# A hand-written instruction order for local and global attention followed by a top-k expert layer

## The chip, the cores and the metric

The kernel runs on one core of a Trainium2 chip. The metric is the device time of one launch in microseconds (us). A core has five engines with an instruction queue each: TensorE (PE, matrix products, with its weight loads shown as PEld), VectorE (DVE), ScalarE (ACT), GpSimd (POOL) and SyncE (SP, which here only issues transfers). Each queue is worked off in order. Transfers (DMA) are issued from SP's and POOL's queues and carried by 16 DMA engines that all queues share. Products land in PSUM, whose buffers here are eight banks; everything else lives in SBUF.

## The reference

Eight batches of eight heads; each head has 512 local positions and 32 global ones of 64 values. Global queries see all keys; a local query sees the 32 global keys and the local keys within 32 positions. The attention's output, 4352 rows of 512, goes through an expert layer: a gate picks one of eight experts per row, each expert keeps its 80 rows of highest gate value, and those rows get `relu(x w1) w2` times the gate; all other rows are zero.

```python
s_g = scale * q_g @ concat(k_g, k_l).T;  out_g = softmax(s_g) @ concat(v_g, v_l)
s_ll = where(abs(i - j) <= 32, scale * q_l @ k_l.T, -1e9)
out_l = softmax(concat(scale * q_l @ k_g.T, s_ll)) @ concat(v_g, v_l)
x = concat(out_g, out_l) as (4352, 512)
expert_idx = argmax(x @ w_gate); gate_w = softmax(x @ w_gate)[expert_idx]
for e in range(8):            # the 80 rows of highest gate_w of this expert
    out[tok_idx] = gate_w[tok_idx] * (relu(x[tok_idx] @ w1[e]) @ w2[e])
```

## The kernel before

The attention goes through 16 quads q: four heads of one batch, two quads to a batch, worked as two head pairs j. For a quad, `load_qk` brings Q and K (cast to fp16 by the transfer, POOL's queue), `regroup` rearranges them on ACT, `T_chunk` turns them on PE into PSUM tag T and ACT copies them to `qkT`; `S_chunk` makes three kinds of scores in PSUM tag S (G: global keys for local queries, gq: global queries, l: the band, 64 local queries against a window of 128 keys) and ACT takes their exp (`eG`, `eQ`, `eL`); DVE and POOL multiply the band's exp by a 0/1 mask `band`, one head each. `H_chunk(q, u)`, four per quad, multiplies with the values into tag O (`o_ps`, two wide products and 16 narrow ones in two passes of fp32), DVE takes the reciprocal and scales into `xn`. `Q_chunk` does the same for global queries, `X_chunk` turns `xn` through tag T into `xT` (ACT copies), and POOL casts `xn` to bf16 (`xb`). Tags T and S have two banks each, O has four. The band's odd windows read values that stand 64 rows lower, so `shift_v` makes a second copy of V by two transfers inside SBUF (SP's queue).

Once per batch, `L_chunk` computes the gate: products of `xT` with the gate's weights, a chain of small DVE steps to the gate value and the chosen expert, the rows written to `x_scr` in DRAM by SP, and a transposition of the scores. The eight batches are put in four groups; when a group is full, the 80 highest scores of each expert are found by `best`: ten rounds of MAX8 and MATCH_REPLACE per list, 53 steps in all ahead of the last merge, which `some(n)` puts between other work.

The expert weights come as pieces of 0.5 MB (cast from fp32 by the transfer, POOL's queue, 4 to an expert). Experts 0 to 2 have room from the start (12 pieces), expert 3 and half of 4 take the buffers of V when its last quads are done (6 pieces), and the other 14 take the attention's memory at its end. `zeros` fills the output with zeros (SP). After the attention come a last top-k of ten rounds, the threshold, the positions and the row indices `idx`; eight gathers of the kept rows (POOL's queue); then the experts one after the other: transpose (`xT`), `h`, relu on ACT, `y`, scaling on DVE, scatter by POOL's queue.

What sets the order: a scheduler. It takes the instructions as the code writes them down, with the loop in the last section of the listing, and reorders each engine's queue by priorities and its own model of time, so that the queues before do not follow the code. The rows of order below show where.

Of the kernel before, what the change touches and what calls it, by code (L numbers as in the profile page):

```python
# [18 lines left out]
P = 128  # L19
WIN = 32  # L20
# [6 lines left out]
def _np_consts(B, S, SG, cap):  # L27
# [6 lines left out]
    for t in range(8):  # L34
        key = 64 * t + p
        band[:, t, :] = (p - i >= 0) & (p - i <= 2 * WIN) & (key >= SG) & (key < S)
# [15 lines left out]
    c["rmask5"] = rm5  # L52
    sel = np.zeros((P, 8), dtype=np.float32)
# [11 lines left out]
def kernel(  # L65
# [14 lines left out]
    nc = tc.nc  # L80
    B, H, SL, D = q_l.shape
# [68 lines left out]

    load_gq(0, 1)
    load_qk(1)
# [36 lines left out]
    shift_v(0)  # L189
    load_gq(1, 8)  # L190
# [37 lines left out]
    def setup_globals(b0, b1):  # L228
        for t, bd in ((1, kbd), (0, qbd)):
            g_ps = psT([P, 4, 128], FP16, f"g_ps{b0}{t}")  # L230
# [506 lines left out]
```

## Time and profile before

| | before |
|---|---|
| device time, median of 3 runs | 368.97 us (365.45 to 370.99) |
| the profiled execution: device time, span | 367.61 us, 365.7 us |
| busy: PE, PEld, DVE, ACT, POOL | 260.6, 189.4, 174.4, 147.9, 147.8 us |
| mean granted clock of TensorE | 0.836 of full speed |
| transfers: POOL's queues (software), SP's (hardware) | 27.72 MB in 48.7%, 31.99 MB in 35.8% of 16 engines' span |

The profile is one execution. A stretch's row gives each engine's busy time with the number of its instructions, then the granted clock and the share of the 16 DMA engines that was busy (over 1 where packets of several queues overlap). A timeline's row gives start, length, engine, line, operation, output and inputs, and in brackets how long the engine idled before it and what it waited for.

### The profile page before, as it was taken

What the parts mean: (1) busy time and instruction counts of PE and PEld (TensorE: products, weight loads), DVE (VectorE), ACT (ScalarE), POOL (GpSimd) and SP (SyncE); (2) the same over time, 40 slices, a digit from 0 to 9 for tenths busy, and PEclk for the clock granted to TensorE, in tenths of its full rate; (3) what the DMA queues carried; (4) which work ended last, traced back from release to release, by engine and by line L of the source; (5) the groups of instructions that cost most, each with busy time, mean ns of one, the idle gap of its engine ahead of it and who ended that gap; (6) DMA issues with size and microseconds to landing.
All of it is one profiled execution on the core that took longest, in us unless ns stands there. A gap on an engine that the chain in (4) does not pass through costs nothing. (4 is left out here: it accounts for less than half of the span.)

```text
span 365.7 us, 8777 instructions
## 1 busy us (share of the span) xinstructions
PE 260.6 (71%) x3510; PEld 189.4 (52%) x3510; DVE 174.4 (48%) x553; ACT 147.9 (40%) x241; POOL 147.8 (40%) x228
## 2 busy tenths in 40 slices
PE   0368888859748989898798989499893302338993
PEld 0246675647436857756666675466671200325661
DVE  3232444606412532519854235994679797501221
ACT  2539464555707474481845647055411000001220
POOL 8814765536411642634234142115334255361211
PEclk9998989988959898898998989799896555556998
DMA  9996999999999997978585265186479999970111
GB/s 150 191 191 112 181 191 242 196 258 216 198 237 219 175 223 220 201 157 172 159 134 171 60 165 143 63 228 142 100 89 243 247 195 210 209 156 21 39 54 36
DMA packets 88601, 60.26 MB, mean 165 GB/s; under 512 B 50544, under 2 KB 79600, under 8 KB 88560
## 3 DMA queue, kind: packets, MB, share of 16 engines
q0 software_dynamic: 35040, 27.72, 48.7%
q1 hardware_dynamic: 53520, 31.99, 35.8%
q8 instruction: 27, 0.44, 0.5%
q14 instruction: 14, 0.11, 0.1%
HBM read 62.19 MB, written 14.70 MB: 210 GB/s over the span
## 5 line engine op out<-in xcount | busy, mean ns | idle before, releaser
L331 PE MATMUL o_ps<-vb,eL 128*64 128x65 f32 x1024 | 73.3, 282 | 12.7 <-DMA vb<-vb 12.7
L331 PEld LDWEIGHTS o_ps<-vb,eL 128*64 128x64 f32 x1024 | 60.3, 184 | 32.6 <-issue 21.2
L307 POOL TENSOR_TENSOR eL<-eL,band 128x512 f32<-128x512 f32 x32 | 43.8, 1369 | 32.9 <-ACT eL L305 32.6
L307 DVE TENSOR_TENSOR eL<-eL,band 128x512 f32<-128x512 f32 x32 | 29.4, 920 | 55.5 <-ACT eL L305 55.5
L366 ACT COPY xT<-x_ps 128x512 f32<-128x512 f32 x32 | 17.3, 589 | 81.1 <-PE x_ps L363 81.1
L325 PE MATMUL o_ps<-vbd,eG 128*128 128x260 f32 x128 | 43.6, 427 | 0.0
L305 ACT ACTIVATE eL<-l_ps 128x512 f32<-128x512 f32 x64 | 36.4, 596 | 14.4 <-PE l_ps L300 14.2
L140 ACT COPY qkr<-qk 128x1024 f16<-128x1024 f16 x32 | 32.6, 1043 | 11.7 <-DMA qk<-in_q_l_dram 8.0
L269 ACT COPY qkT<-T_ps 128x1024 f16<-128x1024 f16 x32 | 31.1, 1015 | 9.6 <-PE T_ps L265 9.6
L691 ACT ACTIVATE hT<-h_ps 128x320 bf16<-128x320 f32 x16 | 6.9, 437 | 63.4 <-PE h_ps L689 63.1
L300 PE MATMUL l_ps<-qkT 64*128 64x64 f16 x512 | 25.2, 194 | 7.9 <-ACT eL L305 5.0
L369 POOL CAST xb<-xn 128x1024 bf16<-128x1024 f32 x16 | 16.6, 1038 | 34.7 <-DVE xn L337 23.9
L300 PEld LDWEIGHTS <-qkT 64*128 64x128 f16 x512 | 18.9, 97 | 20.7 <-issue 18.0
L261 POOL COPY qkT<-kgp 128x32 f16<-128x32 f16 x32 | 8.7, 280 | 47.3 <-PE l_ps L300 47.1
L336 DVE RECIPROCAL rec<-o_ps 128x4 f32<-128x4 f32 x64 | 10.8, 174 | 35.2 <-PE o_ps L331 35.0
L337 DVE TENSOR_TENSOR xn<-o_ps,rec 128x256 f32<-128x256 f32 x64 | 25.1, 411 | 0.7
L325 PEld LDWEIGHTS o_ps<-vbd,eG 128*128 128x128 f32 x128 | 20.6, 200 | 2.6
L133 POOL DMA_DIRECT2D qk<-in_q_l_dram x16 | 12.7, 792 | 22.4 <-ACT qkr L140 15.8
L265 PE MATMUL T_ps<-ident,qkr 128*128 128x128 f16 x256 | 19.7, 225 | 1.4 <-DVE kgp L241 1.3
L363 PE MATMUL x_ps<-identf,xn 128*128 128x128 f32 x128 | 20.2, 288 | 0.0
L265 PEld LDWEIGHTS <-qkr 128*128 128x128 f16 x256 | 16.1, 100 | 4.8 <-issue 3.1
L697 DVE TENSOR_SCALAR y<-y_ps,xg 80x512 f32<-80x512 f32 x8 | 6.0, 747 | 26.3 <-PE y_ps L694 26.3
(137 smaller groups left out, 414.1 us busy)
## 6 DMA issues: line engine op xcount, KB each, us to landing
out_dram<-zt SPq DMA_DIRECT2D x17, 512.0 KB
vb<-vb SPq DMA_DIRECT2D x32, 260.0 KB
w2sb<-in_moe_w_dram POOLq DMA_DIRECT2D x14, 512.0 KB
vb<-in_v_l_dram SPq DMA_DIRECT2D x48, 128.0 KB
w1sb<-in_moe_w_dram POOLq DMA_DIRECT2D x12, 512.0 KB
x_scr<-xb SPq DMA_DIRECT2D x8, 514.0 KB
qk<-in_q_l_dram POOLq DMA_DIRECT2D x16, 256.0 KB
qk<-in_k_l_dram POOLq DMA_DIRECT2D x16, 256.0 KB
```

What stands on the lines that cost most here:

```text
L140: nc.scalar.copy(out=qkr[q][:, t].rearrange("p i h d -> p h i d"), in_=qks[q][:, t])
L265: nc.tensor.transpose(out=T_ps[:, t, 128 * i:128 * i + 128], in_=qkr[q][:, t, i, 2 * j:2 * j + 2, :], identity=ident16[:, :])
L269: nc.scalar.copy(out=dst.rearrange("x t (p i) -> x t p i", i=4), in_=T_ps[:].rearrange("x t (i p) -> x t p i", i=4))
L300: nc.tensor.matmul(out=l_ps[hh][:, 64 * t:64 * t + 64], lhsT=buf[o:o + 64, 512 + 64 * t:640 + 64 * t], rhs=buf[o:o + 64, 64 * t:64 * t + 6 ...
L305: nc.scalar.activation(out=eL[:], in_=l_ps[hh][:], func=AF.Exp, scale=scale)
L307: eng.tensor_tensor(out=eL[:], in0=eL[:], in1=band[:].rearrange("p t i -> p (t i)"), op=ALU.mult)
L325: nc.tensor.matmul(out=o[:].rearrange("p h d -> p (h d)"), lhsT=s["eG"][:, 128 * u:128 * u + 128], rhs=vbd[b % 2][:, qd].rearrange("p h d ...
L331: nc.tensor.matmul(out=o[64 * odd:64 * odd + 64, h, :], lhsT=s["eL"][h][:, 64 * t:64 * t + 64], rhs=v[:, 5 * odd + u, h, :], start=False, ...
L337: nc.vector.tensor_tensor(out=s["xn"][:, u].rearrange("p (h d) -> p h d", h=4), in0=o[:, :, 0:64], in1=rec[:].unsqueeze(2).to_broadcast([P ...
L363: nc.tensor.transpose(out=x_ps[:, 128 * u:128 * u + 128], in_=s["xn"][:, u, 128 * j:128 * j + 128], identity=identf[:, :])
L366: nc.scalar.copy(out=xT[:], in_=x_ps[:])
L369: nc.gpsimd.tensor_copy(out=bs["xb"][:, :, 128 * qd:128 * qd + 128].bitcast(BF16), in_=s["xn"][:])
```

## The change

`tc.manual_schedule()` takes the scheduler away: each engine's queue follows the code. The code is written anew for that. In the loop's pass q, quad q is in its last stage (H, Q, X), quad q+1 has its scores made (L, G and Q fills, mask), quad q+2 is transposed, and Q and K of quad q+3 are regrouped and of q+4 loaded; the pieces of one stage stand between the four H chunks of another. The routing of a finished batch is cut into La, Lb1, Lb2, Lb3, Lc and Ld and spread over one pass, and top-k steps go in by ones and twos: five to a pass, seven from q = 12 on. Weight pieces go out one per pass.

Some work is moved too. Q and K come as fp32 through SP's queue, and ACT casts while it regroups. The shift of V becomes two POOL copies of 64 x 1040 within the same partitions; for that the keys of each odd window stand with their halves exchanged, in a new buffer `kO` that ACT copies from `qkT` (512 columns per head pair), and the mask is exchanged likewise. The copies of `xT` go from ACT to DVE. Small fills of `L` and `oh` on POOL become a product with a constant `valid` on DVE. In the experts, transposes run one expert ahead and `y` one behind.

```diff
+    ctx.enter_context(tc.manual_schedule())
...
-        qks[q] = lpool.tile([P, 2, 4, 4, D], FP16, tag="qk16", bufs=3, name=f"qk16_{q}")
+        qks[q] = lpool.tile([P, 2, 4, 4, D], FP32, tag="qk", name=f"qk{q}")
         for t, src in ((0, q_l), (1, k_l)):
-            nc.gpsimd.dma_start(
+            nc.sync.dma_start(
...
     def shift_v(q):
-        nc.sync.dma_start(out=v[0:64, 5:9], in_=v[64:128, 0:4])
-        nc.sync.dma_start(out=v[64:128, 5:9], in_=v[0:64, 1:5])
+        nc.gpsimd.tensor_copy(out=v[0:64, 5:9], in_=v[0:64, 1:5])
+        nc.gpsimd.tensor_copy(out=v[64:128, 5:9], in_=v[64:128, 0:4])
...
+        nc.scalar.copy(out=kO[(2 * q + j) % 4][:],
+                       in_=buf[:, 576:1088].rearrange("x (u w y) -> x u w y", w=2, y=64)[:, :, ::-1, :])
...
-        nc.scalar.copy(out=xT[:], in_=x_ps[:])
+        nc.vector.tensor_copy(out=xT[:], in_=x_ps[:])
...
     for q in range(NQ):
         b, qd = divmod(q, 2)
+        more = 2 if q >= 12 else 1
+        if q + 4 < NQ:
+            load_qk(q + 4)
         if q + 2 < NQ:
             load_v(q + 2)
+        if q == 4:
+            setup_globals(4, 8)
+        G_chunk(q)
+        H_chunk(q, 0)
+        if q + 2 < NQ:
+            T_chunk(q + 2, 0)
+            kg_copy(q + 2, 0)
+        if pend is not None:
+            La(pend)
+        if q + 1 < NQ:
+            L_fill(q + 1, 0)
+            mask(q + 1, 0)
+        if q + 3 < NQ:
+            regroup(q + 3, 0)
+        if q + 1 < NQ:
             shift_v(q + 1)
+        some(1)
+        H_chunk(q, 1)
+        if pend is not None:
+            Lb1(pend)
+        if q + 1 < NQ:
+            L_fill(q + 1, 1)
+        if q + 2 < NQ:
+            T_chunk(q + 2, 1)
+            kg_copy(q + 2, 1)
+        if pend is not None:
+            Lb2(pend)
+        if q + 1 < NQ:
+            mask(q + 1, 1)
+        some(1)
+        H_chunk(q, 2)
+        if pend is not None:
+            Lb3(pend)
+        some(more)
+        if q + 1 < NQ:
+            G_fill(q + 1)
+            Q_fill(q + 1, 0)
+        if q + 3 < NQ:
+            regroup(q + 3, 1)
+        H_chunk(q, 3)
+        if pend is not None:
+            Lc(pend)
+        some(1)
+        Q_chunk(q)
+        if q + 1 < NQ:
+            Q_fill(q + 1, 1)
+        C_chunk(q)
+        X_chunk(q, 0)
+        X_chunk(q, 1)
+        some(more)
+        if pend is not None:
+            Ld(pend)
+        pend = b if qd == 1 else None
...
+        if q < 4 * NRES:
+            e, k = divmod(q, 4)
             if k == 0:
                 w_tiles(e, wpool)
             load_w(e, (k,))
...
         if q == NQ - 1:
             load_w(NRES, (2, 3))
+            load_w(NRES + 1, (0, 1))
...
+    fx(0)
+    for e in range(E):
+        if e + 1 < E:
+            fx(e + 1)
+        fh(e)
+        if e:
+            fy(e - 1)
+    fy(E - 1)
```

Three places of the order, before and after. The first is ACT's queue in one quad in the middle of the attention, before: T copies (L269), exps of the scores (L293, L286, L305), regroup (L140), xT copies (L366).

```order
L269 COPY qkT_175<-T_ps_0_1939 128x2x512
L269 COPY qkT_176<-T_ps_1_1964 128x2x512
L293 ACTIVATE eQ_0_1996<-gq_ps_0_1990 128x320
L140 COPY qkr_2404<-qk_10_2131 128x4x4x64
L305 ACTIVATE eL_0_0_2016<-l_ps_0_0_1998 128x512
L286 ACTIVATE eG_1988<-G_ps_1987 128x512
L140 COPY qkr_2404<-qk_10_2131 128x4x4x64
L305 ACTIVATE eL_0_1_2019<-l_ps_0_1_1999 128x512
L293 ACTIVATE eQ_1_2043<-gq_ps_1_2037 128x320
L305 ACTIVATE eL_1_0_2063<-l_ps_1_0_2045 128x512
L305 ACTIVATE eL_1_1_2066<-l_ps_1_1_2046 128x512
L366 COPY xT_0_2111<-x_ps_0_2106 128x512
```

The same queue of the change in one pass: L275 is the T copy, L278 the copy to kO, L322 the band's exps, L145 regroup, L293 and L303 the exps of G and gq.

```order
L275 COPY qkT_179<-T_ps_0_2005 128x2x512
L278 COPY kO_183<-qkT_179 128x512
L322 ACTIVATE eL_0_0_2035<-l_ps_0_0_2017 128x512
L322 ACTIVATE eL_0_1_2037<-l_ps_0_1_2018 128x512
L145 CAST qkr_2041<-qk_1723 128x4x4x64
L322 ACTIVATE eL_1_0_2076<-l_ps_1_0_2058 128x512
L322 ACTIVATE eL_1_1_2078<-l_ps_1_1_2059 128x512
L275 COPY qkT_180<-T_ps_1_2080 128x2x512
L278 COPY kO_184<-qkT_180 128x512
L293 ACTIVATE eG_2108<-G_ps_2107 128x512
L303 ACTIVATE eQ_0_2118<-gq_ps_0_2112 128x320
L145 CAST qkr_2041<-qk_1723 128x4x4x64
```

The T copies of the two head pairs are apart now, the first ahead of the exps of the quad before it; the xT copies are gone from ACT, and kO stands in the queue twice.

The second place is DVE's queue while a batch is routed, before: MAX (L461) and MATCH_REPLACE (L463) are the top-k rounds, the other lines the steps of L_chunk.

```order
L393 COPY L<-lg_3973 128x32
L461 MAX R_3819<-cand_3761 8x8
L394 COPY L<-lg_3973 32x8
L463 MATCH_REPLACE cand_3761<-R_3819,cand_3761 8x400
L396 TENSOR_REDUCE lmax<-L 128x5
L461 MAX R_3819<-cand_3761 8x8
L398 TENSOR_TENSOR sh<-L,lmax 128x40
```

The same steps in the change, in pass 14: L420 to L435 are the routing, L357 and L358 the division of H, L329 the band product, L499 and L501 a top-k round.

```order
L420 COPY L_191<-lg_3693 32x8
L422 TENSOR_REDUCE lmax<-L_191 128x5
L424 TENSOR_TENSOR sh<-L_191,lmax 128x40
L428 TENSOR_TENSOR oh<-L_191,lmax 128x40
L431 SCALAR_TENSOR_TENSOR cs<-rmask_148,oh 128x40
L435 SCALAR_TENSOR_TENSOR oh<-cs,oh 128x40
L329 TENSOR_TENSOR eL_1_0_3731<-eL_1_0_3731,band 128x512
L499 MAX R_3739<-cand_3674 8x8
L501 MATCH_REPLACE cand_3674<-R_3739,cand_3674 8x400
L357 RECIPROCAL rec<-o_ps_2_3742 128x4
L358 TENSOR_TENSOR xn_3623<-o_ps_2_3742,rec 128x256
```

Before, half a round stood between any two steps of the routing; now the steps follow each other, and one whole round stands ahead of the next chunk's division.

The third place is POOL's queue at the end of the attention, before: L505 and L509 issue weight pieces, L369 casts xn of a quad to xb.

```order
L505 DMA vb_71<-in_moe_w_dram 128x2x1024
L424 CAST xgb<-xgn_3114 128x128
L307 TENSOR_TENSOR eL_0_1_3651<-eL_0_1_3651,band 128x512
L413 MEMSET oh 32x8
L414 MEMSET oh 64x8
L307 TENSOR_TENSOR eL_1_1_3757<-eL_1_1_3757,band 128x512
L509 DMA vb_72<-in_moe_w_dram 128x4x512
L369 CAST xb_3578<-xn_3579 128x4x256
L509 DMA vb_72<-in_moe_w_dram 128x4x512
L505 DMA vb_70<-in_moe_w_dram 128x2x1024
L369 CAST xb_3578<-xn_3825 128x4x256
```

The same in the change: L543 and L547 issue the pieces, L392 casts, and the second CAST is that of the last quad.

```order
L392 CAST xb_3622<-xn_3623 128x4x256
L485 CAST xgb<-xgn_3155 128x128
L543 DMA vb_73<-in_moe_w_dram 128x2x1024 x2
L392 CAST xb_3622<-xn_3863 128x4x256
L547 DMA vb_74<-in_moe_w_dram 128x4x512 x2
L543 DMA vb_72<-in_moe_w_dram 128x2x1024 x2
L485 CAST xgb<-xgn_3621 128x128
L547 DMA w2sb_4058<-in_moe_w_dram 128x4x512 x2
```

Two pieces of 128x4x512 moved from ahead of the last quad's CAST to behind it; the 14 late pieces follow, as before, and the gathers come behind them in both.

## Rows read from the trace of the kernel before

**Rows 1.** The page's slices: PE's busy tenths and its granted clock.

```profile
PE   0368888859748989898798989499893302338993
...
PEclk9998989988959898898998989799896555556998
```

**Rows 2.** Stretches of one quad each: length, engines' busy time, clock, DMA share, GB/s.

```profile
core 0: us, PE busy (x) PEld busy (x) DVE busy (x) ACT busy (x) POOL busy (x), PEclk, DMA share, GB/s
68.00:89.00 21.00, 15.95 (x230) 12.58 (x229) 7.46 (x27) 9.96 (x17) 10.69 (x16) 0.84 1.19 233
141.00:155.00 14.00, 12.32 (x185) 9.86 (x185) 5.55 (x14) 8.30 (x13) 6.33 (x8) 0.88 0.85 182
155.00:172.40 17.40, 16.02 (x212) 11.26 (x211) 8.85 (x33) 9.14 (x15) 6.29 (x11) 0.90 0.79 167
216.30:240.00 23.70, 18.66 (x220) 12.93 (x219) 16.89 (x61) 9.25 (x15) 4.56 (x10) 0.86 0.41 107
267.60:275.00 7.40, 6.75 (x121) 4.96 (x120) 6.47 (x26) 1.85 (x4) 3.15 (x4) 1.00 0.96 133
```

**Rows 3.** Stretches of one microsecond in a quad, same columns.

```profile
178.00:179.00 1.00, 0.39 (x8) 0.36 (x8) 0.32 (x1) 1.00 (x2) 0.21 (x1) 1.00 0.94 361
179.00:180.00 1.00, 0.26 (x5) 0.20 (x5) 0.28 (x1) 1.00 (x3) 0.00 (x0) 1.00 0.26 102
...
182.00:183.00 1.00, 1.00 (x22) 1.00 (x20) 1.00 (x4) 0.50 (x2) 1.00 (x2) 0.50 0.00 0
```

**Rows 4.** Timeline of PE, in the hole and in two full-clock places.

```profile
179.74 0.31 PE L290 MATMUL gq_ps<-qbd,qkT 128*128 128x64 f16 x5 [1.04 <-ACT eL L305]
180.23 0.80 PE L300 MATMUL l_ps<-qkT 64*128 64x64 f16 x16 [0.18 <-ACT eL L305]
...
242.14 0.66 PE L325 MATMUL o_ps<-vbd,eG 128*128 128x260 f32 x2
...
245.20 1.15 PE L331 MATMUL o_ps<-vb,eL 128*64 128x65 f32 x28
```

**Rows 5.** Timeline from the last quad on: pieces, last X, indices, experts, last y.

```profile
266.69 0.80 POOL L509 DMA_DIRECT2D vb<-in_moe_w_dram  x1 [3.10 <-PE og L347]
...
273.25 1.09 PE L363 MATMUL x_ps<-identf,xn 128*128 128x128 f32 x8
...
317.03 0.16 DVE L666 TENSOR_TENSOR idx<-idf,inv_ps 80x8 uint32<-80x8 f32 x1
...
325.52 0.53 PEld L679 LDWEIGHTS <-xg 80*128 80x128 bf16 x8 [8.82 <-issue]
...
345.60 1.31 PE L689 MATMUL h_ps<-xT,vb 128*128 128x80 bf16 x32 [0.78 <-DVE xT L682]
...
359.52 0.75 DVE L697 TENSOR_SCALAR y<-y_ps,xg 80x512 f32<-80x512 f32 x1 [2.33 <-PE y_ps L694]
```

**Rows 6.** DMA view, 280 to 316 us: packets, MB, share of 16 engines, by queue.

```profile
q0 software_dynamic: 4749, 6.19, 100.3%
q1 hardware_dynamic: 1094, 1.60, 14.2%
```

**Rows 7.** The start: POOL's cast of quad 0, and the first 20 us.

```profile
40.76 1.04 POOL L369 CAST xb<-xn 128x1024 bf16<-128x1024 f32 x1 [1.01 <-DVE xn L337]
...
0.00:20.00 20.00, 3.22 (x24) 2.18 (x24) 5.12 (x28) 7.72 (x8) 15.94 (x39) 1.00 1.33 173
```

**Rows 8.** Groups by line and shape: busy us, mean ns, idle before.

```profile
L305 ACT ACTIVATE eL<-l_ps 128x512 f32<-128x512 f32 x64 | 36.4, 596 | 14.4 <-PE l_ps L300 14.2
...
L269 ACT COPY qkT<-T_ps 128x1024 f16<-128x1024 f16 x32 | 31.1, 1015 | 9.6 <-PE T_ps L265 9.6
...
L369 POOL CAST xb<-xn 128x1024 bf16<-128x1024 f32 x16 | 16.6, 1038 | 34.7 <-DVE xn L337 23.9 <-issue 8.9 <-DVE rg L353 0.9
...
L461 DVE MAX8 R<-cand 8x8 f32<-8x400 f32 x20 | 11.2, 561 | 0.0
```

**Rows 9.** The second half of the attention as one stretch, columns of rows 2.

```profile
141.00:274.30 133.30, 118.24 (x1674) 86.93 (x1673) 77.95 (x263) 67.05 (x111) 45.17 (x64) 0.90 0.63 142
```

**Rows 10.** DVE's band product, 141 to 216 us: ns shortest/median/longest.

```profile
L307 DVE TENSOR_TENSOR eL<-eL,band x10: 683/694/2350, 147.5 to 212.3; 128x512 f32<-128x512 f32 x10
```

More of the change, by code (lines that the diff above doesn't have):

```diff
@@ L34, in _np_consts @@
     for t in range(8):
-        key = 64 * t + p
-        band[:, t, :] = (p - i >= 0) & (p - i <= 2 * WIN) & (key >= SG) & (key < S)
+        w = p if t % 2 == 0 else (p + 64) % P
+        key = 64 * t + w
+        band[:, t, :] = (w - i >= 0) & (w - i <= 2 * WIN) & (key >= SG) & (key < S)
     c["band"] = band
@@ L52, in _np_consts @@
     c["rmask5"] = rm5
+    ok = np.ones((P, NB), dtype=np.float32)
+    ok[SG:, 4] = 0.0
+    c["valid"] = ok
     sel = np.zeros((P, 8), dtype=np.float32)
@@ L184, in shift_v @@
         v = vb[q % 3]
-        nc.sync.dma_start(out=v[0:64, 5:9], in_=v[64:128, 0:4])
-        nc.sync.dma_start(out=v[64:128, 5:9], in_=v[0:64, 1:5])
+        nc.gpsimd.tensor_copy(out=v[0:64, 5:9], in_=v[0:64, 1:5])
+        nc.gpsimd.tensor_copy(out=v[64:128, 5:9], in_=v[64:128, 0:4])
     load_v(0)
-    shift_v(0)
-    load_gq(1, 8)
+    for t in range(2):
+        regroup(0, t)
+    load_qk(1)
     load_v(1)
@@ L453, in L_chunk, with Ld @@
             nc.vector.tensor_copy(out=scT[g][:, k * P:(k + 1) * P], in_=t_ps[:])
-        return g if b == GROUPS[g][-1] else None
+        if g < 3 and b == GROUPS[g][-1]:
+            work.append(best(g))
+    def Ld(b):
+        bs = bst.pop(b)
+        xgb = spool.tile([P, 2, 64], BF16, tag="xgb", name="xgb")
+        nc.gpsimd.tensor_copy(out=xgb[:], in_=bs["xg"][:])
+        xr = x_dram.ap()[b * S:(b + 1) * S, :]
+        nc.sync.dma_start(out=xr[SG:S, :].rearrange("(u p) d -> p u d", p=P), in_=bs["xb"][:])
+        for h4 in range(4):
+            nc.sync.dma_start(
+                out=xr[0:SG, 0:XW - 1].rearrange("g (q f d) -> f g q d", q=2, f=4)[h4],
+                in_=xgb[32 * h4:32 * h4 + 32].bitcast(FP32))
+        nc.sync.dma_start(out=xr[0:SG, XW - 1:XW], in_=bs["gate"][0:SG, 4:5])
     scT, R = {}, {}
@@ L519, in zeros @@
                 nz[0] += 1
-    regroup(0)
-    setup_globals(0, 1)
-    T_chunk(0, 0)
-    T_chunk(0, 1)
-    S_chunk(0, 0)
-    S_chunk(0, 1)
-    pending = None
     work = []
     def some(n):
-        for _ in range(n):
-            if work:
-                try:
-                    next(work[0])()
-                except StopIteration:
-                    work.pop(0)
+        while n and work:
+            try:
+                next(work[0])()
+                n -= 1
+            except StopIteration:
+                work.pop(0)
@@ new lines @@
+    for t in range(2):
+        nc.vector.tensor_copy(out=gq16[:, t], in_=gqf[:, t])
+    T_chunk(0, 0)
+    setup_globals(0, 1)
+    load_qk(2)
+    for t in range(2):
+        regroup(1, t)
+    T_chunk(0, 1)
+    for j in range(2):
+        kg_copy(0, j)
+        L_fill(0, j)
+        mask(0, j)
+    shift_v(0)
+    for j in range(2):
+        T_chunk(1, j)
+        kg_copy(1, j)
+    load_qk(3)
+    G_fill(0)
+    for j in range(2):
+        Q_fill(0, j)
+    for t in range(2):
+        regroup(2, t)
@@ L609 @@
     rpool = ctx.enter_context(tc.tile_pool(name="route", bufs=1, reuse_waits="tile"))
+    xg = [rpool.tile([cap, XW], FP32, name=f"xg{e}") for e in range(E)]
+    for e in range(E):
+        nc.gpsimd.memset(xg[e], 0.0)
     lst = rpool.tile([16, cap], FP32, name="lstf")
@@ L675, with fx @@
                                      bounds_check=N - 1, oob_is_err=False)
-    for e in range(E):
+    xTs, hTs = {}, {}
+    def fx(e):
         xT_ps = psT([P, 4, cap], BF16, f"xT_ps{e}")
```

205 lines of the change are left out of this document (92 added, 113 removed).

## The prediction

> **What bounds the kernel now.** The page's slices come first: PE is 80 to 90% busy through the attention (slices 3 to 30), yet its granted clock keeps falling below full speed, and from slice 31 PE idles while weights still arrive [rows 1]. So there are two stages, the attention up to the last X transposes (274.3 us) and a tail of 91.4 us to the end of the span at 365.7, and I read each by itself.
>
> Attention, the table of one stretch per quad [rows 2]. A quad without routing work takes 14.0 us, one that carries the batch's routing (the L part) 17.4. Busy time times granted clock is PE's work at full speed: 12.32 x 0.88 = 10.8 and 16.02 x 0.90 = 14.4, mean 12.6 of 15.7. The 3.1 us between are a hole and its after-effect, and both are in the one-microsecond stretches: PE is busy for 0.39 and 0.26 of two neighbouring microseconds, and three later the granted clock is 0.50, the lower of its two levels, 1.2 GHz, and the stretch below full speed lasts some 3.3 us [rows 3]. What PE waits for in the hole is ACT: in the timeline a matmul into PSUM tag S waits 1.04 us for the exp that empties a bank of it [rows 4]; S has two banks and every score goes through it. Beside this rhythm three quads are far longer: two of some 21 us, of which one stands in the table, at a DMA share of 1.19 (all 16 engines full), and one of 23.7 us from 216.3 on, where DVE is busy 16.89 us: there the top-k rounds stand between the steps of the L part (the order rows of DVE) [rows 2].
>
> Tail, the timeline from 273 us [rows 5] and the DMA view [rows 6]. Routing has its row indices at 317.2, and the first transposes of gathered rows start only at 325.52. From 280 to 316 POOL's queue alone is busy 100.3% of 16 engines and moves 6.19 MB: weight pieces (0.524 MB each on the side written), 11.8 of them, 3.05 us each. The gathers stand behind them in the same queue. So the experts start when the last weight piece is through, 51.2 us after the attention, for the 16 pieces that POOL issues behind the last quad (16 x 3.05 = 48.8). The experts take 34.0 us to the last y (359.52) and 6.2 us are left for its scatter and the end.
>
> **The change part by part, against the profiled execution** (span 365.7, its time 367.61, which is 1.4 us below the median of the runs shown).
>
> *Start.* The qk loads come as fp32 on SP's queue instead of as a cast on POOL's, and the V shift is a POOL copy instead of two transfers. Before, quad 0 ends with its CAST at 40.8 us, and the first 20 us are DMA-bound (share 1.33) [rows 7]. The second qk pair now waits on SP for regroup(0), since its buffer is shared, and some 18 small loads stand on SP between it and the third pair, which ACT's regroup(2) needs ahead of quad 0's stage for quad 2. I take 42 us for the end of quad 0, bounds 36 (no load waits) and 48 (one regroup late by the 5 to 6 us that three pairs of 1 MB need at the 0.2 MB/us of that stretch).
>
> *Steady quads.* What now stands on PE between two fills of tag S is half of quad q's H work. On ACT the order is T copy, kO copy, two exps (the order rows of ACT). From the last transposes on that is 1.02 + 0.60 (kO has 512 columns, as an exp) + 2 x 0.60 = 2.8 us [rows 8], and I add 0.2 for the handover. PE covers it with the first score fill, 0.80 us, and H(q,1), two wide products (0.66) and 16 narrow ones (28 took 1.15) [rows 4], some 2.0 us together. So a wait of about 1 us stays in each quad; in a routing quad L work covers it, but there a matmul for tag T waits as long for the T copy. I take 1.1. Bounds: no wait, and today's 2 us. Since the wait is half of the old hole and has no second one beside it, I take the clock to stay at its upper level (2.4 GHz): 12.6 + 1.1 = 13.7 us per quad. ACT gains kO and loses xT, two copies of 512 columns each per quad: nothing in the sum. POOL gains two copies of 64x1040 per quad, 1.04 us each by the CAST of 1024 columns [rows 8], bounds 0.9 and 2.1 (as slow as its band product in the worst case), and loses two DMA issues: hidden, since POOL was busy 45.17 us of 133.3 in the second half [rows 9]. The DMA loses the 32 transfers of the shift and nothing else, qk being the same bytes read; the weight pieces come one per quad, where the order before lets POOL issue them as early as buffers allow. That takes away the stretches with share 1.2, and so the two quads of 21 us. On SP the row writes of a batch, which wait for DVE's gates and a POOL cast at a quad's end, now stand ahead of the next qk load; what queues behind them is needed by ACT a quad later, 13 us off, which hides it, and costs PE the delay one to one if they come more than that late.
>
> *Second half, DVE.* It was busy 77.95 us between 141 and 274.3 [rows 9]. It gets 16 xT copies, about 0.6 each (priced by ACT's 512 columns, bounds 0.4 and 0.9), and five more top-k rounds by then, a MAX8 of 0.56 and a replace about as long: 78 + 9.6 + 5.6 = 93 us over 8 quads, 11.7 per quad. That is under 13.7, so DVE doesn't bound, but its queue is in order and each round ahead of a reciprocal holds H's bank. I add 1.5 us to each of the 7 last steady quads, 10 us; bounds 0 and 3 each.
>
> One row speaks against the shift on POOL: the band product on DVE takes 0.69 us in the median and 2.35 at most [rows 10], in stretches where POOL multiplies too. The new copies put 2.1 us more of POOL's SBUF work beside the second band product of each quad. The Trainium skill, "SBUF - State Buffer", section "SBUF: two separate sides", says that a DVE instruction with two SBUF inputs and a GpSimd instruction take one port pair by an exclusive lock, so that the later one waits for the whole of the other. The maximum of that row agrees with it. By the row's median the copies cost nothing, and by the rule 1 to 2 us of DVE per quad. Without the page: if the second product is stretched like the longest one, DVE has 11.7 + 1.7 = 13.4 us per quad, as much as PE; that is a rival below.
>
> So the attention ends at 42 + 14 x 13.7 + 8 (the last quad has no successor; 7.4 before [rows 2], and three rounds more) + 10 = 252 us, against 274.3.
>
> *Tail.* POOL's order decides (the order rows of POOL). Both w2 pieces of expert 3 stand behind the last quad's CAST, where before they went out from 266.7 on [rows 5]: 18 pieces after the attention instead of 16. 18 x 3.05 = 55, plus 1.5 to the first issue, plus 4 for two zero fills and the last rows' write (in the DMA view 1.60 MB of SP's queue took 14.2% of 36 us, 5.1 us [rows 6]; bounds 0 and 5): the experts start 60.5 us after the attention, 9 later than now. Routing doesn't show: by then its 43 us (274.3 to 317.2) are over, even with the seven rounds that are left over for after the L part. The experts in a pipeline lose the waits of PE for xT, 0.78 us per pair of experts and some smaller ones [rows 5]: 34.0 - 2.5 = 31.5. The end stays at 6.2. Together 252 + 60.5 + 31.5 + 6.2 = 350.2 us of span, 352.1 with the 1.9 us around it. The median may lie a microsecond above: I say 352.
>
> **Rivals.**
> 1. *All waits are covered* and DVE's queue holds nobody: 42 + 14 x 12.6 + 8 = 226, so 326, and 340 when half of the waits and of DVE's 10 us stay. For it speaks that PE has work for 12.6 us only [rows 2]; against it the two banks of tag S [rows 4].
> 2. *The clock still falls.* A hole of 1.1 us per quad is enough. Each quad then pays half of 3.3 us at 1.2 GHz, 1.65 x 14 = 23: 375, and 363 when it happens in every second quad. Against it: the rows show the fall behind two microseconds that are two thirds empty [rows 3].
> 3. *POOL's copies hold DVE* (above): DVE at 13.4 us per quad with its queue waits, some 1.5 us more in 8 quads, 12 us: 364.
> 4. *Slower: top-k steps in DVE's queue stop PE.* One mechanism: in the second half a step stands ahead of each reciprocal, H runs out of its four banks, Q and X slip, and the next quad starts late; four routing quads would then cost like the 23.7 us quad, 8.7 more each, 35 us: 387. For it speaks that quad's row; against it that now one or two rounds stand in a place, where there 13 did. It turns the verdict from 3 us on each of the 8 quads.
>
> **How the numbers follow.** Forecast (343 to 361) 0.47; rival 1 0.15; rival 2 0.14; rival 3 0.12; rival 4 0.12. About 2% is what a measurement of this kernel can tell from no change (361.6 to 376.3). Faster: 0.47 + 0.15 + 0.05 of the rivals 2 and 3 = 0.67. Slower: rival 4 and a little of rival 2, 0.14. Same: 0.19. The range 334 to 375 leaves out the fastest part of rival 1 and rival 4; the likeliest case alone is 343 to 361.
>
> **What would show it.** Right: routing and other quads near 15.5 and 12 us in stretches, PEclk 1.0 between 45 and 240 us, a PE wait for ACT of about 1 us at the score fill, no DMA share of 1.2 before 140 us, the last X near 252, the first expert 60 us behind it, and POOL's queue full all that time. Wrong: a clock of 0.5 once per quad (rival 2), a band product on DVE of 1.7 us or more in each quad (rival 3), PE waiting on DVE's reciprocals from quad 8 on (rival 4), or experts that start less than 55 us after the attention.

## The result and the profile after

The changed kernel takes 338.74 us (median of 4 runs, 337.43 to 340.6) against 368.75 us: ratio 0.922, 95% interval 0.913 to 0.930. It is faster, as forecast, and 13 us better than the 352 forecast: inside the range of 334 to 375, but below the 343 to 361 of the likeliest case. Ratios compare runs outside a slower state of the chip; of the four runs with V's shift by DMA (below) only the fastest lies outside it. The profiled execution took 337.43 us; its span is 335.5. By the forecast's own stages:

| stage | forecast, us | measured, us |
|---|---|---|
| quad 0 ends | 42 | 41.9 |
| quads 1 to 7 | 7 x 13.7 = 95.9 | 82.0 |
| quads 8 to 15, to the last X | 95.9 + 8 + 10 = 114 | 119.1 |
| last X to the first expert | 60.5 | 54.8 |
| experts, to the start of the last y | 31.5 | 26.2 |
| from there to the end | 6.2 | 11.4 |

The sum is right to 4%, but with errors of both signs in it: 14 us too much for quads 1 to 7, while the other errors, 5 or 6 us each, cancel almost to nothing. The page's slices of the changed kernel first, which answer to [rows 1]:

```profile
span 335.5 us, 8730 instructions
...
PE   1206989887889889788684878769551013049960
...
PEclk9998699999999999989898599995855555559996
DMA  7787899699899899999879714204999999960211
```

From slice 6 to slice 17 the clock stays up, and PE is busy 70 to 90% (the first eight quads end in slice 15). From slice 18 on both are ragged again. The stretches show the same (columns of [rows 2]: length, busy time of PE, PEld, DVE, ACT and POOL, granted clock, DMA share, GB/s): first the two parts of the attention, then a plain quad and a routing quad of the first, then two routing quads of the second.

```profile
41.90:123.90 82.00, 72.03 (x1358) 52.97 (x1358) 54.30 (x155) 59.74 (x98) 50.05 (x60) 1.00 0.96 224
123.90:243.00 119.10, 91.66 (x1473) 63.96 (x1471) 96.07 (x283) 54.29 (x92) 51.33 (x62) 0.89 0.72 171
...
64.40:75.60 11.20, 10.19 (x221) 7.91 (x210) 6.86 (x18) 8.34 (x14) 7.33 (x10) 1.00 0.96 239
75.60:89.80 14.20, 11.28 (x190) 7.59 (x192) 11.15 (x38) 8.87 (x15) 7.17 (x9) 1.00 1.06 230
150.60:166.50 15.90, 11.60 (x194) 8.18 (x198) 14.00 (x41) 8.62 (x14) 7.08 (x9) 0.95 1.05 265
182.90:201.40 18.50, 15.40 (x206) 10.23 (x206) 13.66 (x44) 9.08 (x15) 6.69 (x8) 0.75 0.52 119
```

In the first part a quad takes 11.7 us, 10.3 of them PE work at full clock. In the second it takes 14.9, with DVE busy 12.0 and no more work for PE (91.66 us at a clock of 0.89, 10.2 per quad). The view of waits names the new holder. The first two rows are PE's waits from 41.9 to 140 us, which is eight quads, the last one those from 140 to 243 (total us, times, longest):

```profile
PE l_ps L318 <- ACT eL L322: 4.0, 8, 0.7
...
PE o_ps L352 <- POOL vb L188: 1.4, 1, 1.4
...
PE x_ps L384 <- DVE xn L358: 11.4, 8, 2.0
```

The tail answers to [rows 5, 6]. The timeline shows the last X transposes, the row indices, the first transposes of gathered rows, the first y and the last y, and the first two scatters and the last; the DMA view is of 243 to 300 us:

```profile
241.69 1.33 PE L384 MATMUL x_ps<-identf,xn 128*128 128x128 f32 x5 [1.94 <-DVE xn L358]
...
286.03 0.16 DVE L751 TENSOR_TENSOR idx<-idf,inv_ps 80x8 uint32<-80x8 f32 x1
...
297.84 0.74 PE L763 MATMUL xT_ps<-identbf,xg 80*128 80x80 bf16 x8 [12.04 <-DMA xg<-x_scr,idx]
...
304.41 0.75 DVE L785 TENSOR_SCALAR y<-y_ps,xg 80x512 f32<-80x512 f32 x1 [2.80 <-PE y_ps L782]
...
324.07 0.75 DVE L785 TENSOR_SCALAR y<-y_ps,xg 80x512 f32<-80x512 f32 x1 [0.98 <-PE y_ps L782]
...
305.44 0.95 POOL L787 DMA_INDIRECT out_dram<-y,idx  x1 [6.26 <-DVE fxT L766]
308.91 0.93 POOL L787 DMA_INDIRECT out_dram<-y,idx  x1 [2.52 <-DVE fxT L766]
...
329.22 0.91 POOL L787 DMA_INDIRECT out_dram<-y,idx  x1 [2.46 <-issue]
```

```profile
q0 software_dynamic: 7801, 10.05, 100.2%
q1 hardware_dynamic: 1208, 1.69, 9.6%
```

The indices are ready 43.2 us after the attention (42.9 before); the gathers land 54.8 us after it, when POOL's queue has moved its 18 pieces. The y's then come every 3.0 us, but the scatters only every 3.4 (8 of them, 305.44 to 329.22), and the last is issued 5.2 us behind the start of its y.

### The profile page after: what moved, and what is told of

Same layout as the page of the kernel before. It is cut to its first block, busy times and chain, and to the rows that moved or that the text cites. A ratio compares the mean times of both kernels' runs of the same rounds, so it can differ in the third digit from the quotient of the medians.

```text
span 335.5 us, 8730 instructions
## 1 busy us (share of the span) xinstructions
PE 218.9 (65%) x3510; PEld 155.6 (46%) x3510; DVE 207.6 (62%) x597; ACT 146.4 (44%) x241; POOL 149.3 (44%) x200
## 5 line engine op out<-in xcount | busy, mean ns | idle before, releaser
L329 POOL TENSOR_TENSOR eL<-eL,band 128x512 f32<-128x512 f32 x32 | 40.9, 1278 | 42.5 <-ACT eL L322 41.0
L329 DVE TENSOR_TENSOR eL<-eL,band 128x512 f32<-128x512 f32 x32 | 27.4, 855 | 41.0 <-ACT eL L322 41.0
L275 ACT COPY qkT<-T_ps 128x1024 f16<-128x1024 f16 x32 | 32.6, 1018 | 42.9 <-PE T_ps L271 37.9
L352 PEld LDWEIGHTS o_ps<-vb,eL 128*64 128x64 f32 x1024 | 37.1, 143 | 26.1 <-issue 20.6
L352 PE MATMUL o_ps<-vb,eL 128*64 128x65 f32 x1024 | 46.5, 234 | 2.4 <-POOL vb L188 1.4
L322 ACT ACTIVATE eL<-l_ps 128x512 f32<-128x512 f32 x64 | 34.7, 597 | 9.6 <-PE l_ps L318 9.6
L145 ACT CAST qkr<-qk 128x1024 f16<-128x1024 f32 x32 | 33.4, 1046 | 12.2 <-DMA qk<-in_q_l_dram 10.7
L777 ACT ACTIVATE fhT<-h_ps 128x320 bf16<-128x320 f32 x16 | 6.9, 437 | 64.0 <-PE h_ps L775 63.6
L392 POOL CAST xb<-xn 128x1024 bf16<-128x1024 f32 x16 | 16.6, 1036 | 29.7 <-DVE xn L358 29.6
L271 PE MATMUL T_ps<-ident,qkr 128*128 128x128 f16 x256 | 22.8, 240 | 10.6 <-ACT qkr L145 7.5
L384 PE MATMUL x_ps<-identf,xn 128*128 128x128 f32 x128 | 22.1, 309 | 11.4 <-DVE xn L358 11.4
L358 DVE TENSOR_TENSOR xn<-o_ps,rec 128x256 f32<-128x256 f32 x64 | 27.2, 425 | 3.2
L318 PE MATMUL l_ps<-qkT 64*128 64x64 f16 x256 | 14.5, 200 | 16.1 <-POOL qkT L283 10.0
L384 PEld LDWEIGHTS x_ps<-identf,xn 128*128 128x128 f32 x128 | 15.8, 156 | 13.9 <-DVE xn L358 13.5
L387 DVE COPY xT<-x_ps 128x512 f32<-128x512 f32 x32 | 20.6, 684 | 2.2 <-PE x_ps L384 1.9
L187 POOL COPY vb<-vb 64x1040 f32<-64x1040 f32 x16 | 17.0, 1062 | 10.4 <-DMA vb<-in_v_l_dram 10.4
L303 ACT ACTIVATE eQ<-gq_ps 128x320 f32<-128x320 f32 x32 | 13.9, 435 | 16.6 <-PE gq_ps L300 16.5
L318 PEld LDWEIGHTS <-qkT 64*128 64x128 f16 x256 | 10.2, 99 | 22.9 <-issue 11.2
```

What stands on the lines that cost most here:

```text
L187: nc.gpsimd.tensor_copy(out=v[0:64, 5:9], in_=v[0:64, 1:5])
L271: nc.tensor.transpose(out=T_ps[:, t, 128 * i:128 * i + 128], in_=qkr[q][:, t, i, 2 * j:2 * j + 2, :], identity=ident16[:, :])
L275: nc.scalar.copy(out=dst.rearrange("x t (p i) -> x t p i", i=4), in_=T_ps[:].rearrange("x t (i p) -> x t p i", i=4))
L318: nc.tensor.matmul(out=l_ps[hh][:, 64 * t:64 * t + 64], lhsT=lhsT, rhs=buf[o:o + 64, 64 * t:64 * t + 64], start=True, stop=True)
L322: nc.scalar.activation(out=eL[:], in_=l_ps[hh][:], func=AF.Exp, scale=scale)
L329: eng.tensor_tensor(out=eL[:], in0=eL[:], in1=band[:].rearrange("p t i -> p (t i)"), op=ALU.mult)
```

## The experiments

Each runs the changed kernel with the edit shown; times are medians with lowest and highest, ratios are against the kernel before on the same chip. By stage, in the profiled execution of each:

| run | to last X | to first expert | from there to end | first scatter behind first expert |
|---|---|---|---|---|
| changed kernel | 243.0 | 54.8 | 37.7 | 7.6 |
| without the fixed order | 269.1 | 49.6 | 44.5 | 12.9 |
| xT on ACT | 239.5 | 55.0 | 38.8 | 8.4 |
| places behind each move | 228.3 | 58.4 | 43.8 | 13.4 |
| w2 of expert 3 early | 248.8 | 51.9 | 39.3 | 9.0 |
| tail edits | 244.5 | 45.4 | 44.5 | 14.1 |
| attention edits | 229.4 | 55.3 | 38.1 | 8.1 |
| both | 227.8 | 48.5 | 46.9 | 14.0 |
| both, gathers spread | 229.0 | 48.5 | 41.1 | 9.3 |

**The order alone.**

```diff
-    ctx.enter_context(tc.manual_schedule())
```

> The changed kernel with the line taken out that holds each engine to the written order; the code and all data paths (V shift on POOL, fp32 qk loads on SP, the two odd-block copies, xT on DVE) stay. Theory A, the order itself pays: with another order on PE and ACT quads 1 to 7 go from 11.7 us back to 13.5 or more, the granted clock falls below 1.00 in most quads, attention ends at 262 or later, the whole takes 355 or more. Theory B, the data paths pay: quads 1 to 7 stay within 0.4 us of 11.7 and the whole is under 345.

Measured 364.79 us (364.51 to 365.76), ratio 0.989 (0.985 to 0.994). Theory A: with these data paths, 26 of the 30 us are the order's. The slice row of the clock, and two stretches, quads 2 to 7 and quads 8 to 15:

```profile
PEclk9999999969999989899789969969995555557995
```

```profile
63.85:155.44 91.59, 80.47 (x1255) 57.62 (x1252) 52.48 (x143) 64.11 (x103) 41.81 (x51) 0.93 0.79 213
155.44:269.10 113.66, 96.04 (x1477) 71.42 (x1475) 84.89 (x266) 53.40 (x91) 52.46 (x59) 0.91 0.52 133
```

Quad 1 ends at 63.85 us, not 52.7 (PE once waits 9.8 us for a transfer of global values, ahead of 41.24 us), and quads 2 to 7 take 15.3 us each, not 11.9. The clock falls less often than theory A had it (0.93, slices 9, 15 and 17). In the second half, however, 113.7 us stand against 119.1: there the written order is no better than the scheduler's. By its place the gain is all in the start, the first half and the experts.

**Score matmuls head by head.**

```diff
-        for t in range(8):
-            for hh in range(2):
+        for hh in range(2):
+            for t in range(8):
```

> The changed kernel with the 16 small score matmuls of a fill issued head by head (8 and 8), not in turns between the two heads. In the trace 16 in turns take some 0.40 us (two at once, on the two halves of TensorE's rows), while in the kernel before 8 of one head took 0.40. Theory A, part of my over-sized PE work is this: the fills take 0.8 us each, PE busy grows by 0.8 us per quad, quads 1 to 7 go from 11.7 to 12.3 or more, the second half (paced by DVE) stays, the whole goes from 338.7 to 342 to 345. Theory B, ACT's chain paces the first half: nothing beyond 1 us changes.

Measured 338.19 us (337.37 to 340.21), ratio 0.917 (0.911 to 0.923): theory B. Quads 1 to 7 take 81.6 us:

```profile
41.90:123.46 81.56, 73.28 (x1348) 54.12 (x1347) 53.74 (x153) 59.60 (x98) 49.82 (x61) 1.00 0.96 225
```

PE is busy 1.3 us longer in these seven quads, 0.2 each and not 0.8, and it goes into the wait for ACT at the same fill. The price of taking turns between the heads was not what I had over-sized.

**The V shift by DMA again.**

```diff
-        nc.gpsimd.tensor_copy(out=v[0:64, 5:9], in_=v[0:64, 1:5])
-        nc.gpsimd.tensor_copy(out=v[64:128, 5:9], in_=v[64:128, 0:4])
+        nc.sync.dma_start(out=v[0:64, 5:9], in_=v[0:64, 1:5])
+        nc.sync.dma_start(out=v[64:128, 5:9], in_=v[64:128, 0:4])
```

> The changed kernel with the V shift put back as two SBUF-to-SBUF transfers per quad (here on SP's queue) in place of the two POOL copies. Theory A, the shift's transfers were what made PE wait in the kernel before (12.7 us in 3 waits between 40.8 and 155 us): the DMA share of the first half rises above 1.1, PE waits 8 us or more for vb, the whole takes 346 to 352. Theory B, one weight piece per quad leaves the transfers room: PE waits under 2 us for vb and the whole stays within 2 us of 338.7.

Measured 383.63 us (374.93 to 389.8) against 369.49 (366.76 to 370.75). By its waits theory A, and beyond its numbers; its DMA share above 1.1 did not come (0.92 from 43.8 to 140.4 us). The run to compare is the fastest, 374.93; the profile is of the one of 386.2. PE's waits from 42 to 291 us in it, and the largest entry of SP's:

```profile
PE o_ps L352 <- DMA vb<-vb: 38.7, 8, 8.8
...
SPq L487 <- DVE xb L454: 45.3, 6, 16.4
```

With this fixed order PE stood eight times for a late transfer. SP's queue, in which the transfers stand, waits for the row writes of a batch, while the DMA share is below that of the kernel before (1.14 from 40.8 to 155 us): that points at the queue, but no run took transfer time and queue apart. So order and data path need each other: V's old data path in the new order is not faster than the kernel before (374.93 at best, one run), and the new data paths in the scheduler's order gain 1%, too little to count as a change. The other moved work (Q and K through SP, `kO`, `valid`, the experts' code) was not undone one by one.

**No top-k step in the quads.**

```diff
     def some(n):
+        if n < 9:
+            return
```

> The changed kernel with no top-k step between the parts of the quads: all 53 steps run after the last routing part. Theory A, the steps in DVE's queue are what makes quads 8 to 15 take 14.75 us each against 11.7: attention ends near 221 instead of 243 (12 us per quad); the 44 steps that move cost some 45 us on DVE behind it plus two waits for a transfer, so the whole takes some 365. Theory B, the second half is slow for something else (xT on DVE, POOL beside DVE, the clock): attention ends at 238 or later and the whole takes 380 or more.

Measured 374.23 us (2 runs). The attention ends at 223.2, quads 8 to 15 take 12.5 us each (expected 12): theory A for the attention. The whole misses its 365.

```profile
123.50:223.20 99.70, 87.08 (x1473) 62.35 (x1471) 55.52 (x168) 54.66 (x92) 50.84 (x61) 0.91 0.86 192
```

The steps in DVE's queue therefore cost the second half 119.1 - 99.7 = 19.4 us. Behind the attention they cost more, since there nothing covers them: the indices come 102 us after it.

**xT on ACT, and empty places behind the move.** Two ways to take some 11.5 us from DVE's second half.

```diff
-        nc.vector.tensor_copy(out=xT[:], in_=x_ps[:])
+        nc.scalar.copy(out=xT[:], in_=x_ps[:])
```

> The changed kernel with the xT copy (128x512, 0.68 us on DVE, two per quad) put back on ACT. Theory A, DVE's total load paces the second half: DVE loses 1.3 us per quad, quads 8 to 15 go from 14.75 to 13.7 us each, and the attention ends near 235 instead of 243; the first half may lose up to 4 us since ACT's copies and exps are what its score fills wait for; the whole 331 to 336. Theory B, not the load but the places of the top-k steps in DVE's queue stop PE: the second half changes by less than 3 us, and the whole is 337 or more.

```diff
             yield move
+            for _ in range(6):
+                yield lambda: None
```

> The changed kernel with six empty places put between the move of a group's candidates (a transfer on SP's queue) and the first top-k step that reads them. Theory A: the one wait of 4.46 us in which DVE stands before 173.98 us for that transfer, with everything behind it in its queue, goes, and the attention ends 3 to 5 us earlier; the six steps that this leaves for the tail hide there, where routing is done 11.8 us before the gathers have landed; the whole 334 to 336. Theory B: the time returns at the next steps, since DVE has its work to do in any case, and the whole stays within 1.5 us of 338.7.

Measured 335.98 us (334.99 to 339.73), ratio 0.918 (0.909 to 0.927), and 333.71 us (332.37 to 336.69), ratio 0.911 (0.903 to 0.919). The second half of the attention in the one and the other:

```profile
123.00:239.50 116.50, 92.49 (x1473) 64.78 (x1471) 84.90 (x267) 63.89 (x109) 51.22 (x62) 0.88 0.73 172
```

```profile
123.50:228.30 104.80, 85.23 (x1473) 60.39 (x1470) 84.34 (x252) 54.31 (x92) 51.11 (x61) 0.95 0.77 178
```

DVE is busy 84 to 85 us in both, 11 to 12 less than in the changed kernel. Without the xT copies that is worth 2.6 us, with the places 14.3; they leave 30 top-k rounds there instead of 41. So DVE's load alone does not pace the second half; what stands in its queue ahead of H's reciprocals does more. The xT theory B held for the second half (2.6 us, under its 3), while the whole came out 1 us below its bound, inside theory A's 331 to 336. The gap gave 14.7 us in the attention, more than its theory A said (3 to 5), and two thirds went back: 3.6 us by the longer routing and 6.1 behind the first expert. The one wait that the gap removes is this one of the changed kernel, a transfer on SP's queue for which DVE stood, and with it everything behind:

```profile
173.98 0.57 DVE L499 MAX8 R<-cand 8x8 f32<-8x400 f32 x1 [4.46 <-DMA cand<-lst]
```

The quad around it shrank from 16.4 to 10.6 us, and the last quad, with two rounds instead of eight, from 11.9 to 7.4. With xT on ACT the same wait grew to 7.5 us, so it took back part of what the copies had freed.

**Two pieces out of the tail.**

```diff
-            load_w(NRES, (0, 1))
+            load_w(NRES, (0, 1, 2, 3))
         if q == NQ - 1:
-            load_w(NRES, (2, 3))
```

> The changed kernel with both w2 pieces of expert 3 issued at the end of the last quad but one, as before the change, so that 16 and not 18 weight pieces stand behind the last quad. Theory A, POOL's queue sets when the experts start: they start 2 x 3.05 = 6.1 us sooner (48.7 us after the attention, against 54.8), the whole 332 to 333.5. Theory B, routing and the gathers' own transfers set it: under 2 us.

Measured 338.71 us (336.86 to 341.9), ratio 0.920 (0.913 to 0.927): no gain. The tail did get 2.9 us shorter, but in the profiled execution, the longest of the four, the attention was 5.8 us longer with the same instructions up to its last quads. Inconclusive by itself; the tail edits below ask it again.

**Every second scatter left out** (the rows of experts 0, 2, 4 and 6 stay zero).

```diff
+        if e % 2 == 0:
+            return
         nc.gpsimd.indirect_dma_start(out=out,
```

> The changed kernel without the scatters of experts 0, 2, 4 and 6 (their rows of the output stay zero). Theory A, the scatters run one behind the other, 3.4 us each, and set the end: with every second one gone the last follows its y at once (324.8 us in the trace), the span ends near 331, the whole is 333 to 335. Theory B, the experts' matmuls set the end: the last scatter comes where it did, the whole stays within 1.5 us of 338.7.

Measured 334.11 us (2 runs), span 331.5; the last y starts at 324.89 us and the last scatter is issued at 325.92. Theory A: the chain of scatters sets the end.

**Tail edits, attention edits, both.** Tail: w1 of expert 3 a quad earlier, its w2 behind the last quad but one, and the w2 pieces of expert 7 behind the gathers (the added line stands there):

```diff
-        load_w(e, (2, 3))
+        if e < E - 1:
+            load_w(e, (2, 3))
...
+    load_w(E - 1, (2, 3))
```

> The changed kernel with other places for eight weight pieces only: w1 of expert 3 goes out a quad earlier, its w2 behind the last quad but one, and the two w2 pieces of expert 7 behind the gathers in POOL's queue. So 14 pieces stand between the attention and the gathers, not 18. Theory A, POOL's queue sets the experts' start until routing does: 14 x 3.05 = 43 us, routing 43 us and 3.3 us for a gather to land; the experts start 46.5 us behind the attention and not 54.8, the whole takes 330 to 331. Theory B, the transfers that leave the tail lengthen the attention by as much: the attention ends at 247 or later, the whole takes 335 or more.

Attention: xT on ACT as above, four places behind the move, and

```diff
-GROUPS = [[0, 1, 2, 3], [4, 5], [6], [7]]
+GROUPS = [[0, 1, 2], [3, 4, 5], [6], [7]]
```

> The changed kernel with three edits to the attention: xT on ACT, groups of three and three batches for the first two top-k lists instead of four and two (the first list's steps begin two quads earlier), four empty places behind each move of candidates. The tail is left. Theory A, quads 8 to 15 are as long as DVE's queue makes them: DVE loses 10 us by the copies and some 12 us of steps to the quads 6 to 8, so the second half goes from 119 us to some 100 and the attention ends near 225; the experts still start 54.8 us behind it, by POOL's queue; the whole takes 318 to 323. Theory B, something else paces the second half too: the attention ends at 233 or later and the whole takes 328 or more.

> The edits of the tail and of the attention together. Theory A: the attention ends near 225, behind it routing decides (43 us, four more top-k steps of 1.05 us, 3.3 us for a gather): the experts start at 275, the whole takes 313 to 317. Theory B, the 14 pieces hold the gathers again, or the pieces moved forward slow the last quads: the whole takes 320 or more.

Measured: tail 336.85 us (336.19 to 338.73), ratio 0.916 (0.909 to 0.923); attention 325.66 us (322.14 to 326.86), ratio 0.883 (0.873 to 0.892); both 325.59 us (323.93 to 326.32), ratio 0.883 (0.876 to 0.890). All three totals miss theory A (330 to 331, 318 to 323 and 313 to 317); the first and the last lie where their theories B had them, but not for those reasons (the attention ends at 244.5 us, and the 14 pieces do not hold the gathers). The attention's edits do most of what was expected of them (229.4 us, not 225). The tail's bring the first expert to 45.4 us, as theory A said (46.5), and yet nearly nothing: the experts give it back. PE in the run with the tail edits alone, and one row each of DVE and ACT:

```profile
291.48 2.33 PE L778 MATMUL h_ps<-fxT,w1sb 128*128 128x80 bf16 x32
293.88 1.07 PE L778 MATMUL h_ps<-fxT,w1sb 128*128 128x80 bf16 x13
295.70 0.43 PE L778 MATMUL h_ps<-fxT,w1sb 128*128 128x80 bf16 x4 [0.75 <-issue]
297.14 0.49 PE L778 MATMUL h_ps<-fxT,w1sb 128*128 128x80 bf16 x5 [1.00 <-issue]
298.57 0.83 PE L778 MATMUL h_ps<-fxT,w1sb 128*128 128x80 bf16 x10 [0.94 <-issue]
299.19 3.61 PE L785 MATMUL y_ps<-w2sb,fhT 128*80 128x512 bf16 x8
...
298.69 0.33 DVE L769 COPY fxT<-xT_ps 128x320 bf16<-128x320 bf16 x1 [6.64 <-remote]
...
298.63 1.24 ACT L780 ACTIVATE fhT<-h_ps 128x320 bf16<-128x320 f32 x3 [3.84 <-remote]
```

Expert 1's products stand in three gaps that no semaphore in the profile explains, in the time in which POOL issues the last gathers (287.17 to 297.1); then y runs at half clock (3.61 us, 1.90 later). PE is not alone: DVE's copy and ACT's relu start 4.6 and 4.8 us after PE had finished their inputs (294.1 and 293.8 us), with no releaser but "remote". In the changed kernel PE starts only when the gathers are nearly all issued, and has no such gap.

**The gathers spread**, on top of both (`gather(e)` is the indirect transfer of one expert's rows).

```diff
-    for e in range(E):
+    for e in range(5):
         gather(e)
...
             fy(e - 1)
+            if e + 4 < E:
+                gather(e + 4)
```

> The kernel with the edits of the tail and of the attention, and the gathers of experts 5, 6 and 7 moved behind the scatters of experts 0, 1 and 2 in POOL's queue, so that POOL issues five gathers and not eight while the first experts run. In the run with both edits the experts started 5.5 us sooner behind the attention than in the one with the attention's edits alone, but the first scatter came 14.0 us behind their start instead of 8.1: the matmuls of expert 1 stand in three gaps of 0.8 to 1.0 us for which the profile names no releaser, while POOL still issues gathers. Theory A, what holds PE there goes with the gathers: three fewer shorten it by some 3.8 us, the first scatter comes 10 to 11 us behind the start, the whole takes 320 to 323. Theory B, the gaps belong to the first experts whatever POOL does: the first scatter comes 13.5 us or more behind the start and the whole stays within 1.5 us of 325.6.

Measured 322.68 us (320.36 to 325.74), ratio 0.877 (0.868 to 0.886). Theory A: PE's gaps are gone, and DVE's copy follows PE at once, at 281.98 us; ACT's first relu still starts 3.0 us behind the start of its products (1.3 in the changed kernel).

```profile
279.08 2.33 PE L783 MATMUL h_ps<-fxT,w1sb 128*128 128x80 bf16 x32
281.21 0.47 PE L771 MATMUL xT_ps<-identbf,xg 80*128 80x80 bf16 x4
281.48 2.33 PE L783 MATMUL h_ps<-fxT,w1sb 128*128 128x80 bf16 x32
283.61 2.06 PE L790 MATMUL y_ps<-w2sb,fhT 128*80 128x512 bf16 x8
```

The first scatter comes 9.3 us behind the first expert instead of 14.0. So the gaps hang on when POOL issues the three gathers (the two pieces behind them moved forward with that, and one execution of each was profiled); by which way they hold PE, DVE and ACT is open. This is the fastest version found by its median, and its interval lies below that of the changed kernel. Against the run with both edits the whole gains 2.9 us, with ranges that overlap.

## Why the prediction was right, and which steps were off

*Quads 1 to 7 (14 us too long).* The failed step is "Busy time times granted clock is PE's work at full speed ... mean 12.6"; measured are 10.3, and 2.3 in seven quads is more than the whole error. The pair of stretches it used was too high. Quads 1 to 7 as one stretch of the kernel before give 94.03 x 0.87 / 7 = 11.7:

```profile
40.80:155.00 114.20, 94.03 (x1345) 70.23 (x1344) 43.28 (x136) 60.82 (x97) 53.51 (x80) 0.87 1.14 215
```

and [rows 9], nine quads and not eight, gives 118.24 x 0.90 / 9 = 11.8. So the choice of stretch explains 0.9 of the 2.3. The rest is the method: busy time times clock is not fixed work, for the same products took less in the changed kernel, 72.03 / 7 = 10.3. The largest part is H's narrow products, of the same number and shape, before and after (busy us of the whole kernel, mean ns, idle before):

```profile
L331 PE MATMUL o_ps<-vb,eL 128*64 128x65 f32 x1024 | 73.3, 282 | 12.7 <-DMA vb<-vb 12.7
...
L352 PE MATMUL o_ps<-vb,eL 128*64 128x65 f32 x1024 | 46.5, 234 | 2.4 <-POOL vb L188 1.4
```

In quads 1 to 7 they were busy 34.17 us before and 19.21 after. Part of that is the clock, which was low just where they stood: multiplied by the granted clock of each half microsecond, the 34.17 are 24.4, and the other 5.2 us are 0.7 per quad. The scores l and G and the gate's products lost 0.4 to 0.5 per quad each, by the same count (busy times overlap, so these do not add up exactly). At the gate it can be seen: before, its eight products of a batch stood in two lots (the first two rows), now in one (the third, of the changed kernel), for half the time. Why the other products cost less was not tested.

```profile
159.06 1.04 PE L380 MATMUL lt_ps<-xT,wg 128*32 128x512 f32 x2
...
160.38 1.06 PE L380 MATMUL lt_ps<-xT,wg 128*32 128x512 f32 x6
```

```profile
55.06 1.07 PE L403 MATMUL lt_ps<-xT,wg 128*32 128x512 f32 x8 [0.38 <-DVE xgT L400]
```

The other half of that step was right: the wait at the score fill is there (0.5 us a quad by the view of waits, all idle time 1.4, forecast 1.1), and the clock stays up, but only to 124 us and not to 240. Rival 2 is out for these quads; in the second half the clock fell again (0.75 in one quad), and what that alone cost was not taken apart. Rival 1 comes near with its 340, but by luck: PE's waits are there, and DVE's queue holds. The shift on POOL took 1.04 to 1.05 us a copy in the median, as priced, and cost PE 1.4 us once. But I priced the removed transfers only by the DMA share; the 12.7 us that PE waited for them in three waits of the first half of the kernel before I had not looked up, and the third experiment shows what hangs on them.

*Quads 8 to 15 (5 us too short).* The mechanism was right, "each round ahead of a reciprocal holds H's bank"; its term was mis-sized. The steps cost 19.4 us, not 10 (2.4 per quad, within the bounds of 0 and 3). Of these, 4.5 us are DVE's wait for the moved candidates, which the forecast did not list. How the rest divides is not shown: spread evenly over 41 rounds, the wait and eleven rounds would be worth 8.5 us, and the gap gave 14.3 in this half. The base came out at 99.7 us without steps, against 103.9, which hid nearly half of the error. The load argument ("11.7 per quad. That is under 13.7, so DVE doesn't bound") named the wrong quantity: with equal loads, 84 to 85 us, the second halves differ by 11.7 us. It also divided the load of nine quads [rows 9] by eight; by nine it is 10.4, measured are 12.0. Rival 4 is this same mechanism, at a lower price than it asked.

*Rival 3* is real and small. DVE's band product takes 0.69 us in the median and 1.45 at most, 27.4 us in 32 where 32 x 0.69 is 22.1: 5 us in the whole kernel, and the longest is shorter than the 2.35 of [rows 10]. Before, the same 32 took 29.4 us, so the new copies made it no worse.

*Tail (5.7 us too long).* "plus 1.5 to the first issue, plus 4": 18 x 3.05 = 55 is the whole wait, since the first piece goes out at 242.68 us, before the last X is done. SP's 1.69 MB went beside the pieces, as [rows 6] had already shown, where the two queues' shares add up to 114%.

*Experts and end (37.7 forecast, 37.7 measured, by chance).* The pipeline saves 7.8 us, not 2.5: an expert takes 3.0 us. "The end stays at 6.2" failed: with y every 3.0 us the scatters, 3.4 each, become the bound, and 5.2 us come back at the end.

## What to carry to other kernels

Size an engine's work from the whole of a stage, not from two stretches next to each other, and where the clock was low in it expect less once the order changes (11.7 against 10.3 here); and price a step in an in-order queue by what stands behind it, not by its share of the load. When a stage gets faster, look up the rate of the next chain behind it (here the scatters, 3.4 us each against 3.0), and count waits for transfers from the waits view even where the DMA share seems to explain them. A fixed order paid here where every producer was early by design; with V's late transfers in it PE waited 38.7 us for them, against 12.7 in the kernel before.

## What the runs showed of the hardware

A small DVE instruction can last as long as the POOL instruction beside it. Three DVE rows and two POOL rows of the changed kernel:

```profile
221.16 0.19 DVE L428 TENSOR_TENSOR oh<-L,lmax 128x40 f32<-128x40 f32 x1
221.38 1.00 DVE L431 TENSOR_TENSOR_SCAN cs<-rmask,oh 128x40 f32<-128x40 f32 x1
222.42 1.28 DVE L435 SCALAR_TENSOR_TENSOR oh<-cs,oh 128x40 f32<-128x40 f32 x1
...
221.24 1.05 POOL L188 COPY vb<-vb 64x1040 f32<-64x1040 f32 x1
222.38 1.27 POOL L329 TENSOR_TENSOR eL<-eL,band 128x512 f32<-128x512 f32 x1
```

The scan (0.24 us elsewhere) and the product behind it (0.20 elsewhere) both have two SBUF inputs and end with POOL's instruction. The Trainium skill, "SBUF — State Buffer", section "SBUF: two separate sides", says that such a DVE instruction and a GpSimd one that reads SBUF take a shared port pair as an exclusive lock; these rows agree with it.

The other surprise is PE's three gaps of 0.75 to 1.0 us without a releaser while POOL issued gathers, with DVE and ACT standing 4.6 and 4.8 us beside them; PE's gaps and DVE's wait went when three of eight gathers were issued later.
